# One table function for GELU, and two 64-row matmuls side by side, in a spectral block with a GEGLU feed-forward

## The chip, the cores and the metric

The kernel runs on one core of a Trainium2 chip. The metric is the device time of one execution in microseconds (us), lower is better. The engines are PE (TensorE, matmuls; its weight loads are listed as PEld), DVE (VectorE), ACT (ScalarE), POOL (GpSimd) and SP (SyncE, which here only issues DMAs).

## The reference

Two blocks in sequence, on x of shape 1 x 2048 x 576 in bf16. The first mixes tokens and features with a 2-D Fourier filter; the second is a feed-forward network with a gated GELU.

```python
def _gelu(x):
    return jax.nn.gelu(x, approximate=True)

def _A_ref(x, w_r, w_i):          # S = 2048, D = 576
    X = rfft2(x.astype(float32))
    X = X * (w_r + 1j * w_i)
    return irfft2(X, s=(S, D)).astype(bfloat16)

def _B_ref(x, w_gate, w_up, w_down):   # F = 4608
    return (_gelu(x @ w_gate) * (x @ w_up)) @ w_down

h  = x + _A_ref(_layernorm(x), A_w_r, A_w_i)
h2 = h + _B_ref(_layernorm(h), B_w_gate, B_w_up, B_w_down)
```

The approximate GELU is the tanh form. It equals g times the sigmoid of a cubic in g, which is how the kernel before computes it.

## The kernel before

The kernel is written with a tile framework. The program order is a list of priorities: a scheduler decides the order on each engine ahead of time, allots buffers, inserts the waits, and picks the engine of `nc.any` copies. So instructions of one stage can stand among those of another.

**Stage A, to 178 us.** Tables of sines and cosines are built, x is normalised and transposed, and the Fourier transforms are done as matmuls and DVE butterflies. At the start SP loads x into `h_sb` (L71, four pieces) and the first nine column blocks of the gate weights into `wg_pre` (L84); POOL loads those of the up weights into `wu_pre` (L85). As 576 features are four and a half times 128, the weights have five row blocks (`dt` 0 to 4) and the fifth has only 64 rows. Rows 64 to 127 of the fifth block are set to zero by POOL (L79, L80), so that the fifth matmul may use all 128 rows.

**LN stage, 178 to about 234 us.** For each of the 16 token groups `s2` of 128 tokens: the last inverse transform (`y_ps`, L667 to L690, partly with 33 rows, since 289 frequencies are 128 + 128 + 33), the sum into `h_sb` (L701), the statistics on ACT (L93, L97), the square root on ACT (L111), the normalised row `hrow` on DVE (L710), and five transposes on PE (`pt`, L722), the fifth with 64 columns. Copies (L723) bring these into `hlnT`, which holds the normalised activations with features on partitions. Rows 64 to 127 of its fifth block were set to zero at the start (L73).

**FFN, from 228 us to the end.** Four token chunks `tcnk` of 512 tokens. For each, a loop over the 36 column blocks `f` of 128 hidden features:

- five matmuls of 128 rows, 128 columns and 512 tokens into `gate_ps` (L793), five more into `up_ps` (L801); each of the two has two PSUM buffers;
- GELU in four steps: Square on ACT into `t_sb` (L809), DVE (t + 1/c) times gate into `z_sb` (L811), Sigmoid on ACT into `s_sb` (L815), DVE gate times s (L818);
- times `up_ps` on DVE into `P_sb` (L819).

Then the down projection: eight accumulators `acc` of 288 columns (four groups of 128 tokens, two halves), each over 36 matmuls (L826), and a sum into `h_sb` on DVE (L833). In the order that the scheduler made, some fifty of the 288 down matmuls of a chunk stand between the gate and up matmuls. A buffer of `gate_ps` is given back by L818, one of `up_ps` by L819.

The weights are streamed again for each token chunk, in pieces of up to nine `f`, into two buffers `wg_c` and `wu_c`. For each piece POOL first sets rows 64 to 127 of the fifth block to zero (L757, L758); SP then issues the gate loads (L766, L770) and POOL the up loads (L771, L775). In the first token chunk the pieces are shorter (9, 1, 3, 5, 9 and 9 blocks), and the down weights `wd_sb` (L783) are loaded in it too.

Of the kernel before, what the change touches and what calls it, by code (L numbers as in the profile page):

```python
# [10 lines left out]
ACT = mybir.ActivationFunctionType  # L11
ALU = mybir.AluOpType
FP32 = mybir.dt.float32
BF16 = mybir.dt.bfloat16

P = 128
S = 2048
S2 = 16
D = 576
# [3 lines left out]
DT_SIZES = [128, 128, 128, 128, 64]  # L23
NDT = 5
# [3 lines left out]
GELU_C1 = 2.0 * math.sqrt(2.0 / math.pi)  # L28
GELU_C3 = 0.044715
# [7 lines left out]
def kernel_body(  # L37
# [12 lines left out]
    nc = tc.nc  # L50
# [25 lines left out]
    NPRE = 9  # L76
    wg_pre = xpool.tile([P, NDT, NPRE * P], BF16, name="wg_pre")
    wu_pre = xpool.tile([P, NDT, NPRE * P], BF16, name="wu_pre")
    nc.gpsimd.memset(wg_pre[64:128, NDT - 1, :], 0.0)  # L79
    nc.gpsimd.memset(wu_pre[64:128, NDT - 1, :], 0.0)  # L80
    for dt in range(NDT):
        Kd = DT_SIZES[dt]
        d0 = dt * P
        nc.sync.dma_start(wg_pre[:Kd, dt, :], B_w_gate[d0 : d0 + Kd, 0 : NPRE * P])  # L84
        nc.gpsimd.dma_start(wu_pre[:Kd, dt, :], B_w_up[d0 : d0 + Kd, 0 : NPRE * P])  # L85
    sumsA = small.tile([P, S2], FP32, name="sumsA")
    sumsqA = small.tile([P, S2], FP32, name="sumsqA")
    sumsB = small.tile([P, S2], FP32, name="sumsB")
# [31 lines left out]
    with tc.tile_pool(name="consts", bufs=1) as consts:  # L120
# [230 lines left out]
        with (  # L351
# [262 lines left out]
            with (  # L614
# [30 lines left out]
                for s2 in range(S2):  # L645
                    B2r = bpool.tile([P, NJT, P], BF16, name="B2r", tag="B2r")
                    B2i = bpool.tile([P, NJT, P], BF16, name="B2i", tag="B2i")
                    Gc = G3[:, s2, 0, :]
                    Gs = G3[:, s2, 1, :]
                    Gns = G3[:, s2, 2, :]  # L650
                    for jt in range(1, NJT):
                        Mj = JT_SIZES[jt]
                        j0 = jt * P
                        ur = Ar[:, s2, j0 : j0 + Mj]
                        ui = Ai[:, s2, j0 : j0 + Mj]
                        b2r_ps = psB.tile([P, P], FP32, name="b2r_ps", tag="b2r_ps")
                        b2i_ps = psB.tile([P, P], FP32, name="b2i_ps", tag="b2i_ps")
                        nc.tensor.matmul(b2r_ps[:Mj, :], lhsT=ur, rhs=Gc, start=True, stop=False)  # L658
                        nc.tensor.matmul(b2r_ps[:Mj, :], lhsT=ui, rhs=Gns, start=False, stop=True)  # L659
                        nc.tensor.matmul(b2i_ps[:Mj, :], lhsT=ur, rhs=Gs, start=True, stop=False)  # L660
                        nc.tensor.matmul(b2i_ps[:Mj, :], lhsT=ui, rhs=Gc, start=False, stop=True)
                        nc.any.tensor_copy(B2r[:Mj, jt, :], b2r_ps[:Mj, :])  # L662
                        nc.any.tensor_copy(B2i[:Mj, jt, :], b2i_ps[:Mj, :])
                    for c in range(2):
                        c0 = c * (D // 2)
                        y_ps = psB.tile([P, D // 2], FP32, name="y_ps", tag="y_ps")
                        nc.tensor.matmul(  # L667
                            y_ps[:],
                            lhsT=b2a[:, s2, 0, :],
                            rhs=CDp[:, 0, c0 : c0 + D // 2],  # L670
                            start=True,
                            stop=False,
                        )
                        nc.tensor.matmul(
                            y_ps[:],
                            lhsT=b2a[:, s2, 1, :],
                            rhs=SDp[:, 0, c0 : c0 + D // 2],
                            start=False,
                            stop=False,
                        )  # L680
                        for jt in range(1, NJT):
                            Mj = JT_SIZES[jt]
                            nc.tensor.matmul(  # L683
                                y_ps[:],
                                lhsT=B2r[:Mj, jt, :],
                                rhs=CDp[:Mj, jt, c0 : c0 + D // 2],
                                start=False,
                                stop=False,
                            )
                            nc.tensor.matmul(  # L690
                                y_ps[:],
                                lhsT=B2i[:Mj, jt, :],
                                rhs=SDp[:Mj, jt, c0 : c0 + D // 2],
                                start=False,
                                stop=(jt == NJT - 1),
                            )
                        if "y" in dbg:
                            ydbg = bpool.tile([P, D // 2], FP32, name="ydbg", tag="ydbg")
                            V.tensor_copy(ydbg[:], y_ps[:])
                            nc.sync.dma_start(dbg["y"][:, s2, c0 : c0 + D // 2], ydbg[:])  # L700
                        V.tensor_tensor(  # L701
                            h_sb[:, s2, c0 : c0 + D // 2],
                            h_sb[:, s2, c0 : c0 + D // 2],
                            y_ps[:],
                            ALU.add,
                        )
                    ln_stats(h_sb, s2, sumsB, sumsqB, hpool)
                    rstd1, nmr1 = ln_scalars(sumsB, sumsqB, s2, s2 + 1, hpool)
                    hrow = hpool.tile([P, D], BF16, name="hrow", tag="hrow")
                    V.tensor_scalar(  # L710
                        hrow[:],
                        h_sb[:, s2, :],
                        rstd1[:, s2 : s2 + 1],
                        nmr1[:, s2 : s2 + 1],
                        op0=ALU.mult,
                        op1=ALU.add,
                    )
                    for dt in range(NDT):
                        Kd = DT_SIZES[dt]
                        d0 = dt * P  # L720
                        pt = psT.tile([P, P], BF16, name="pt", tag="pt")
                        nc.tensor.transpose(pt[:Kd, :], hrow[:, d0 : d0 + Kd], ident[:])  # L722
                        nc.any.tensor_copy(hlnT[:Kd, dt, s2 * P : (s2 + 1) * P], pt[:Kd, :])  # L723
    if "h" in dbg:
        nc.sync.dma_start(dbg["h"], h_sb[:])
    if "hlnT" in dbg:
# [2 lines left out]
    with (  # L729
# [14 lines left out]
        for tcnk in range(4):  # L744
# [5 lines left out]
            for qi, (fa, fb) in enumerate(chunks):  # L750
# [3 lines left out]
                if not skip_load:  # L754
                    wg_c = wgpool.tile([P, NDT, FQ * P], BF16, name="wg_c", tag="wg_c")
                    wu_c = wgpool.tile([P, NDT, FQ * P], BF16, name="wu_c", tag="wu_c")
                    nc.gpsimd.memset(wg_c[64:128, NDT - 1, : nfq * P], 0.0)  # L757
                    nc.gpsimd.memset(wu_c[64:128, NDT - 1, : nfq * P], 0.0)  # L758
                    g0 = 0
                    while g0 < nfq:  # L760
                        g1 = min(g0 + 3, nfq)
# [10 lines left out]
                            wu_c[:, 0:4, lc0:lc1],  # L772
                            B_w_up[0 : 4 * P, gc0:gc1].rearrange("(dt k) c -> k dt c", k=P),
                        )
                        nc.gpsimd.dma_start(wu_c[:64, 4, lc0:lc1], B_w_up[4 * P : D, gc0:gc1])  # L775
                        g0 = g1
                if not wd_loaded and (tcnk > 0 or qi >= 1):
                    wd_loaded = True
# [5 lines left out]
                for fi in range(nfq):  # L784
# [4 lines left out]
                        wgs, wus, fi2 = wg_c, wu_c, fi  # L789
                    gate_ps = psG.tile([P, 4 * P], FP32, name="gate_ps", tag="gate_ps")  # L790
                    up_ps = psG.tile([P, 4 * P], FP32, name="up_ps", tag="up_ps")
                    for dt in range(NDT):
                        nc.tensor.matmul(  # L793
                            gate_ps[:],
                            lhsT=wgs[:, dt, fi2 * P : (fi2 + 1) * P],
                            rhs=hlnT[:, dt, tok0 : tok0 + 512],
                            start=(dt == 0),
                            stop=(dt == NDT - 1),
                        )
                    for dt in range(NDT):  # L800
                        nc.tensor.matmul(  # L801
                            up_ps[:],
                            lhsT=wus[:, dt, fi2 * P : (fi2 + 1) * P],
                            rhs=hlnT[:, dt, tok0 : tok0 + 512],
                            start=(dt == 0),
                            stop=(dt == NDT - 1),
                        )
                    t_sb = gpool.tile([P, 4 * P], BF16, name="t_sb", tag="t_sb")
                    nc.scalar.activation(t_sb[:], gate_ps[:], ACT.Square)  # L809
                    z_sb = gpool.tile([P, 4 * P], FP32, name="z_sb", tag="z_sb")  # L810
                    V.scalar_tensor_tensor(  # L811
                        z_sb[:], t_sb[:], 1.0 / GELU_C3, gate_ps[:], op0=ALU.add, op1=ALU.mult
                    )
                    s_sb = gpool.tile([P, 4 * P], BF16, name="s_sb", tag="s_sb")
                    nc.scalar.activation(  # L815
                        s_sb[:], z_sb[:], ACT.Sigmoid, bias=zerob[:], scale=GELU_C1 * GELU_C3
                    )
                    V.tensor_tensor(s_sb[:], gate_ps[:], s_sb[:], ALU.mult)  # L818
                    V.tensor_tensor(P_sb[:, f, :], s_sb[:], up_ps[:], ALU.mult)  # L819
            for st in range(4):  # L820
                s2 = tcnk * 4 + st
# [67 lines left out]
```

## Time and profile before

| | before |
|---|---|
| median of 6 runs | 699.7 us (697.57 to 700.83) |
| the profiled execution | 700.78 us, span 699.0 us |
| granted TensorE clock, mean | 0.938 |
| PE busy | 585.2 us, 84% |
| DVE busy | 478.0 us, 68% |
| ACT busy | 302.5 us, 43% |
| POOL busy | 127.2 us, 18% |

The span runs from the first to the last instruction; the execution's own time is 1.8 us longer. In a row of the profile, L793 is line 793 of the kernel; then come the engine, the operation, out<-in, the shape (for PE rows*columns of the array, then rows x columns that are streamed), the count, the busy time in us, the mean duration of one in ns, and the idle time before it with what ended it. In a timeline the first two numbers are the start and the duration in us. Matmuls are pipelined: the duration is a latency, and the distance from one start to the next is what a matmul takes of the engine.

### The profile page before, as it was taken

Reading aid. Unit: us, or ns where it says so; the run is one execution under the profiler, and the core shown is the slowest. Engines: PE = TensorE matmul, PEld = TensorE weight load, DVE = VectorE, ACT = ScalarE, POOL = GpSimd, SP = SyncE. Lnnn points to the kernel's source line nnn. Section 1 sums busy time; section 2 is a strip of 40 time slices with the busy share of each in tenths; the row PEclk is TensorE's granted clock in tenths of the full one; section 3 lists DMA queues with packets and bytes.
Section 4 is the critical chain, followed back from the end, with each engine's and each line's share of the span. In section 5 each row is a group of like instructions: output and inputs, shape, how many; then the busy total and the mean of one; then the engine's idle time right before and its main releaser. Section 6 shows DMA issues by size and latency. Waiting matters only on the chain.

```text
span 699.0 us, 9591 instructions
## 1 busy us (share of the span) xinstructions
PE 585.2 (84%) x3470; PEld 327.7 (47%) x3502; DVE 478.0 (68%) x1008; ACT 302.5 (43%) x713; POOL 127.2 (18%) x181
## 2 busy tenths in 40 slices
PE   0069980202999999999999999999999999999997
PEld 0037740201455444447744445754444674444475
DVE  5984699999577888882188886148888416878810
ACT  6753591200677655550055553025555104555500
POOL 8910000000000335312002333003213300330000
PEclk9999965655699999999999999999999999999999
DMA  9500000000000958335005553103345500540000
GB/s 309 101 14 1 1 2 0 1 0 0 1 1 1 325 160 246 91 97 149 35 2 152 152 153 97 57 35 99 86 121 153 153 1 35 152 138 17 0 2 34
DMA packets 45294, 55.48 MB, mean 79 GB/s; under 512 B 8992, under 2 KB 37936, under 8 KB 45248
## 3 DMA queue, kind: packets, MB, share of 16 engines
q1 hardware_dynamic: 36720, 29.80, 14.9%
q0 software_dynamic: 8528, 25.08, 12.1%
q8 instruction: 27, 0.44, 0.3%
q14 instruction: 19, 0.16, 0.1%
HBM read 52.50 MB, written 2.36 MB: 78 GB/s over the span
## 4 chain that ended last, share of the span: by engine, by line
DVE 46%; PE 34%; ACT 16%; issue 2%; DMA 1%; DVEq 0%; SPq 0%; ACTq 0%
PE acc L826 17%; ACT s_sb L815 14%; DVE s_sb L818 13%; DVE z_sb L811 12%; DVE P_sb L819 5%; PE gate_ps L793 2%; PE y_ps L683 2%; PE pt_x L345 2%; PE ar_ps L370 2%; PE y_ps L690 2%; PE ai_ps L378 1%; PE up_ps L801 1%; PE pt L722 1%; PE y_ps L667 1%; DMA h_sb<-in_A_x_dram 1%
## 5 line engine op out<-in xcount | busy, mean ns | idle before, releaser
L793 PE MATMUL gate_ps<-hlnT,wg_c 128*128 128x512 bf16 x660 | 166.3, 379 | 3.7 <-DVE s_sb L818 0.5
L801 PE MATMUL up_ps<-hlnT,wu_c 128*128 128x512 bf16 x661 | 166.3, 379 | 0.5
L815 ACT ACTIVATE s_sb<-z_sb,zerob 128x512 bf16<-128x512 f32 x144 | 104.0, 722 | 141.5 <-DVE z_sb L811 141.5
L826 PE MATMUL acc<-wd_sb,P_sb 128*128 128x288 bf16 x1152 | 156.7, 286 | 0.7
L818 DVE TENSOR_TENSOR s_sb<-gate_ps,s_sb 128x512 bf16<-128x512 f32 x144 | 99.6, 692 | 57.4 <-ACT s_sb L815 57.4
L826 PEld LDWEIGHTS <-P_sb 128*128 128x128 bf16 x1152 | 112.1, 98 | 43.5 <-DVE P_sb L819 2.9
L809 ACT ACTIVATE t_sb<-gate_ps 128x512 bf16<-128x512 f32 x144 | 85.1, 591 | 105.8 <-PE gate_ps L793 103.2
L757 POOL MEMSET wg_c<- 64x1152 bf16 (+3 forms) x17 | 16.0, 940 | 492.7 <-issue 302.6
L793 PEld LDWEIGHTS <-wg_c 128*128 128x128 bf16 x675 | 65.7, 97 | 81.2 <-issue 10.8
L819 DVE TENSOR_TENSOR P_sb<-s_sb,up_ps 128x512 bf16<-128x512 bf16 x144 | 98.3, 683 | 5.3
L801 PEld LDWEIGHTS <-wu_c 128*128 128x128 bf16 x675 | 66.0, 98 | 76.6 <-issue 1.3
L811 DVE SCALAR_TENSOR_TENSOR z_sb<-t_sb,gate_ps 128x512 f32<-128x512 bf16 x144 | 98.4, 683 | 4.5 <-ACT t_sb L809 3.9
L833 DVE TENSOR_TENSOR h_sb<-h_sb,acc 128x288 bf16<-128x288 bf16 x32 | 14.5, 454 | 102.3 <-PE acc L826 102.3
L345 PE MATMUL pt_x<-ident,xn 128*128 128x128 bf16 (+1 forms) x80 | 14.0, 293 | 40.9 <-DVE xn L256 36.4
L658 PE MATMUL b2r_ps<-G_105,Ar 128*128 128x128 bf16 (+1 forms) x32 | 7.9, 247 | 42.8 <-DVE Ar L547 42.8
L771 POOL DMA_DIRECT2D wu_c<-in_B_w_up_dram x46 | 35.3, 768 | 1.4 <-issue 1.4
L345 PEld LDWEIGHTS <-xn 128*128 128x128 bf16 (+1 forms) x80 | 7.5, 128 | 47.2 <-DVE xn L256 36.4
L662 ACT CAST B2r<-b2r_ps 128x128 bf16<-128x128 f32 (+1 forms) x22 | 5.8, 263 | 49.1 <-PE b2r_ps L659 48.9
L658 PEld LDWEIGHTS <-Ar 128*128 128x128 bf16 (+1 forms) x32 | 3.2, 100 | 47.5 <-DVE Ar L547 43.0
L775 POOL DMA_DIRECT2D wu_c<-in_B_w_up_dram x46 | 25.0, 544 | 0.0
L564 POOL DMA_DIRECT2D wi_all<-in_A_w_i_dram x32 | 23.1, 730 | 2.1 <-DMA wu_pre<-in_B_w_up_dram 1.0
L701 DVE TENSOR_TENSOR h_sb<-h_sb,y_ps 128x288 bf16<-128x288 bf16 x32 | 14.4, 451 | 11.2 <-PE y_ps L690 10.8
(396 smaller groups left out, 675.7 us busy)
## 6 DMA issues: line engine op xcount, KB each, us to landing
wg_c<-in_B_w_gate_dram SPq DMA_DIRECT2D x44, 384.0 KB, 5.2
wu_c<-in_B_w_up_dram POOLq DMA_DIRECT2D x44, 384.0 KB, 7.4
wd_sb<-in_B_w_down_dram SPq DMA_DIRECT2D x2, 1296.0 KB, 14.3
wd_sb<-in_B_w_down_dram POOLq DMA_DIRECT2D x2, 1296.0 KB, 11.7
h_sb<-in_A_x_dram SPq DMA_DIRECT2D x4, 576.0 KB, 5.8
out_dram<-h_sb SPq DMA_DIRECT2D x4, 576.0 KB, 2.8
wu_c<-in_B_w_up_dram POOLq DMA_DIRECT2D x44, 48.0 KB, 6.9
wg_c<-in_B_w_gate_dram SPq DMA_DIRECT2D x44, 48.0 KB, 4.8
```

Of the source, the lines that this page charges most:

```text
L345: nc.tensor.transpose(pt[:Kd, :], xn[:, s2, d0 : d0 + Kd], ident[:])
L564: nc.gpsimd.dma_start(wi_all[:, p, :], A_w_i[k2 * P : (k2 + 1) * P, ja:jb])
L771: nc.gpsimd.dma_start(wu_c[:, 0:4, lc0:lc1], B_w_up[0 : 4 * P, gc0:gc1].rearrange("(dt k) c -> k dt c", k=P),)
L775: nc.gpsimd.dma_start(wu_c[:64, 4, lc0:lc1], B_w_up[4 * P : D, gc0:gc1])
L793: nc.tensor.matmul(gate_ps[:], lhsT=wgs[:, dt, fi2 * P : (fi2 + 1) * P], rhs=hlnT[:, dt, tok0 : tok0 + 512], start=(dt == 0), stop=(dt == ...
L801: nc.tensor.matmul(up_ps[:], lhsT=wus[:, dt, fi2 * P : (fi2 + 1) * P], rhs=hlnT[:, dt, tok0 : tok0 + 512], start=(dt == 0), stop=(dt == ND ...
L809: nc.scalar.activation(t_sb[:], gate_ps[:], ACT.Square)
L811: V.scalar_tensor_tensor(z_sb[:], t_sb[:], 1.0 / GELU_C3, gate_ps[:], op0=ALU.add, op1=ALU.mult)
L815: nc.scalar.activation(s_sb[:], z_sb[:], ACT.Sigmoid, bias=zerob[:], scale=GELU_C1 * GELU_C3)
L818: V.tensor_tensor(s_sb[:], gate_ps[:], s_sb[:], ALU.mult)
L819: V.tensor_tensor(P_sb[:, f, :], s_sb[:], up_ps[:], ALU.mult)
L826: nc.tensor.matmul(acc[:], lhsT=P_sb[:, f, st * P : (st + 1) * P], rhs=wd_sb[:, f, cc0 : cc0 + D // 2], start=(f == 0), stop=(f == NFT - 1),)
```

## The change

GELU becomes one table function on ACT, `Gelu_apprx_tanh`, read from `gate_ps` and written to `s_sb`; Square, the two DVE steps and Sigmoid go. The gate's 64-row rest stays in rows 0 to 63 of the fifth weight block, the up's is loaded into rows 64 to 127, and no rows are set to zero for the weights any more. `hrow` is widened to 640 columns, and a DVE copy repeats its last 64 features, so that the fifth transpose gives 128 rows: features 512 to 575 twice, in rows 0 to 63 and 64 to 127 of `hlnT`'s fifth block. The first two matmuls of each `f` are then the two 64-row rests, gate in the upper half of the array's rows and up in the lower half, and eight 128-row matmuls follow.

```diff
-    nc.gpsimd.memset(wg_pre[64:128, NDT - 1, :], 0.0)
-    nc.gpsimd.memset(wu_pre[64:128, NDT - 1, :], 0.0)
     for dt in range(NDT):
...
-        nc.gpsimd.dma_start(wu_pre[:Kd, dt, :], B_w_up[d0 : d0 + Kd, 0 : NPRE * P])
+        uo = 64 if dt == NDT - 1 else 0
+        nc.gpsimd.dma_start(wu_pre[uo : uo + Kd, dt, :], B_w_up[d0 : d0 + Kd, 0 : NPRE * P])
...
-                    hrow = hpool.tile([P, D], BF16, name="hrow", tag="hrow")
+                    hrow = hpool.tile([P, NDT * P], BF16, name="hrow", tag="hrow")
                     V.tensor_scalar(
-                        hrow[:],
+                        hrow[:, 0:D],
...
+                    V.tensor_copy(hrow[:, D : NDT * P], hrow[:, 4 * P : D])
                     for dt in range(NDT):
-                        Kd = DT_SIZES[dt]
                         d0 = dt * P
                         pt = psT.tile([P, P], BF16, name="pt", tag="pt")
-                        nc.tensor.transpose(pt[:Kd, :], hrow[:, d0 : d0 + Kd], ident[:])
-                        nc.any.tensor_copy(hlnT[:Kd, dt, s2 * P : (s2 + 1) * P], pt[:Kd, :])
+                        nc.tensor.transpose(pt[:], hrow[:, d0 : d0 + P], ident[:])
+                        nc.any.tensor_copy(hlnT[:, dt, s2 * P : (s2 + 1) * P], pt[:])
...
-                    nc.gpsimd.memset(wg_c[64:128, NDT - 1, : nfq * P], 0.0)
-                    nc.gpsimd.memset(wu_c[64:128, NDT - 1, : nfq * P], 0.0)
...
-                        nc.gpsimd.dma_start(wu_c[:64, 4, lc0:lc1], B_w_up[4 * P : D, gc0:gc1])
+                        nc.gpsimd.dma_start(wu_c[64:128, 4, lc0:lc1], B_w_up[4 * P : D, gc0:gc1])
...
-                    for dt in range(NDT):
+                    fs = slice(fi2 * P, (fi2 + 1) * P)
+                    ts = slice(tok0, tok0 + 512)
+                    nc.tensor.matmul(
+                        gate_ps[:], lhsT=wgs[0:64, 4, fs], rhs=hlnT[0:64, 4, ts], start=True, stop=False
+                    )
+                    nc.tensor.matmul(
+                        up_ps[:], lhsT=wus[64:128, 4, fs], rhs=hlnT[64:128, 4, ts], start=True, stop=False
+                    )
+                    for dt in range(4):
                         nc.tensor.matmul(
...
+                            gate_ps[:], lhsT=wgs[:, dt, fs], rhs=hlnT[:, dt, ts], start=False, stop=(dt == 3)
+                        )
+                    for dt in range(4):
                         nc.tensor.matmul(
...
+                            up_ps[:], lhsT=wus[:, dt, fs], rhs=hlnT[:, dt, ts], start=False, stop=(dt == 3)
+                        )
-                    t_sb = gpool.tile([P, 4 * P], BF16, name="t_sb", tag="t_sb")
-                    nc.scalar.activation(t_sb[:], gate_ps[:], ACT.Square)
-                    z_sb = gpool.tile([P, 4 * P], FP32, name="z_sb", tag="z_sb")
-                    V.scalar_tensor_tensor(
-                        z_sb[:], t_sb[:], 1.0 / GELU_C3, gate_ps[:], op0=ALU.add, op1=ALU.mult
-                    )
                     s_sb = gpool.tile([P, 4 * P], BF16, name="s_sb", tag="s_sb")
-                    nc.scalar.activation(
-                        s_sb[:], z_sb[:], ACT.Sigmoid, bias=zerob[:], scale=GELU_C1 * GELU_C3
-                    )
-                    V.tensor_tensor(s_sb[:], gate_ps[:], s_sb[:], ALU.mult)
+                    nc.scalar.activation(s_sb[:], gate_ps[:], ACT.Gelu_apprx_tanh, bias=zerob[:], scale=1.0)
                     V.tensor_tensor(P_sb[:, f, :], s_sb[:], up_ps[:], ALU.mult)
```

More of the change, by code (lines that the diff above doesn't have):

```diff
@@ L791, in kernel_body @@
                     up_ps = psG.tile([P, 4 * P], FP32, name="up_ps", tag="up_ps")
-                    for dt in range(NDT):
[L793 to L798, printed above, removed]
+                    fs = slice(fi2 * P, (fi2 + 1) * P)
+                    ts = slice(tok0, tok0 + 512)
@@ L799, in kernel_body @@
                         )
-                    for dt in range(NDT):
+                    for dt in range(4):
                         nc.tensor.matmul(
[L802 to L806, printed above, removed]
-                        )
-                    t_sb = gpool.tile([P, 4 * P], BF16, name="t_sb", tag="t_sb")
```

## The prediction

> **What bounds the kernel now.** I read the page first, for the groups that cost most.
>
> ```profile
> PE 585.2 (84%) x3470; PEld 327.7 (47%) x3502; DVE 478.0 (68%) x1008; ACT 302.5 (43%) x713; POOL 127.2 (18%) x181
> ...
> L793 PE MATMUL gate_ps<-hlnT,wg_c 128*128 128x512 bf16 x660 | 166.3, 379 | 3.7 <-DVE s_sb L818 0.5
> L801 PE MATMUL up_ps<-hlnT,wu_c 128*128 128x512 bf16 x661 | 166.3, 379 | 0.5
> ...
> L818 DVE TENSOR_TENSOR s_sb<-gate_ps,s_sb 128x512 bf16<-128x512 f32 x144 | 99.6, 692 | 57.4 <-ACT s_sb L815 57.4
> ```
>
> The FFN (gate, up, GELU, down) runs from 228 us to the end. PE's 379 ns is the latency of one pipelined matmul, so its occupancy has to be read from start to start. The chain of waits puts most of the loop on DVE and ACT, as if the GELU set its pace; the table of windows (PE, PEld, DVE, ACT, POOL, clock, DMA share, GB/s) speaks against that: PE has hardly a gap, DVE is busy for 63%.
>
> ```profile
> 178.00:228.00 50.00, 49.52 (x350) 25.52 (x349) 33.76 (x168) 37.55 (x142) 0.48 (x3) 0.92 0.01 1
> 345.00:462.00 117.00, 115.63 (x647) 63.72 (x655) 73.25 (x116) 46.25 (x72) 23.82 (x32) 1.00 0.33 97
> ```
>
> The timeline of PE then shows what is lost inside the loop:
>
> ```profile
> 403.92 0.41 PE L826 MATMUL acc<-wd_sb,P_sb 128*128 128x288 bf16 x2
> 404.39 1.24 PE L793 MATMUL gate_ps<-hlnT,wg_c 128*128 128x512 bf16 x5
> 405.47 0.29 PE L826 MATMUL acc<-wd_sb,P_sb 128*128 128x288 bf16 x1
> 405.59 1.24 PE L801 MATMUL up_ps<-hlnT,wu_c 128*128 128x512 bf16 x5
> ```
>
> Five 512-column matmuls take 1.08 us (404.39 to 405.47), 0.216 each; a 288-column one takes 0.12. Down-projection matmuls fill places where PE would wait. Two of them end at 404.16, but the gate starts at 404.39: gate_ps has two buffers, and the older one is free only after DVE's third GELU step (L818). The list of waits has it as
>
> ```profile
> ACT s_sb L815 <- DVE z_sb L811: 141.5, 143, 1.5
> PEld L793 <- issue: 11.4, 44, 0.4
> ```
>
> The long first line costs nothing (ACT is not the bound); the second, 11.4 us in 44 waits of 0.25, is time that PE loses.
>
> The check by sums: one token chunk lasts from 345.85 to 462.07, 116.2 us. It holds 360 x 0.216 = 77.8 us of gate and up and 288 x 0.123 = 35.4 of down (0.123 from 28.6 us for 232 in the chain), 113.2 together. So only 3.0 us per chunk, 12 in all, is waiting; the rest is PE's own work. The five-step GELU is late by a hair, not by its length.
>
> Last, what a change of tile shape costs PE. The LN stage already has 33-row matmuls between 128-row ones, and 64-column transposes:
>
> ```profile
> 205.04 0.30 PE L667 MATMUL y_ps<-CDp,b2a 128*128 128x288 bf16 x1
> 205.26 0.24 PE L722 MATMUL pt<-ident,hrow 128*64 128x128 bf16 x1
> 205.44 0.30 PE L674 MATMUL y_ps<-SDp,b2a 128*128 128x288 bf16 x1
> 205.57 0.29 PE L683 MATMUL y_ps<-CDp,B2r 128*128 128x288 bf16 x1
> 205.69 0.29 PE L690 MATMUL y_ps<-SDp,B2i 128*128 128x288 bf16 x1
> 205.91 0.29 PE L683 MATMUL y_ps<-CDp,B2r 33*128 33x288 bf16 x1
> 206.14 0.30 PE L667 MATMUL y_ps<-CDp,b2a 128*128 128x288 bf16 x1
> ```
>
> Equal shapes: 205.57 to 205.69, 0.12. Into 33 rows: 0.22. Out again: 0.23. Each change costs 0.10 us.
>
> **The change, part by part.** Everything is summed against the profiled execution, 700.78 us (span 699.0), which is 1.1 above the median of 699.7.
>
> *GELU.* Per f it removes the Square on ACT (591 ns), two DVE passes (683 and 692) and the Sigmoid (722), and adds one Gelu from PSUM, bounded by the two ACT rows at 0.6 to 0.72. None of this lies on PE. What it buys is gate_ps: free 0.7 us after the gate's last matmul instead of 3. DVE and ACT then need 0.7 us each in a 2.16 us period; PE stops waiting. That returns the 12 us of waits, less a remnant: **-11.0** (bounds -8 to -12.5). Next late is nothing but PE. The down matmuls used as fillers move to the end of the chunk, at the same price.
>
> *The row pair.* Two 64-row matmuls replace two 128-row ones. If they run side by side, one 0.216 disappears: 144 x 0.216 = -31.1. But the tile shape changes twice per f: 144 x 0.20 = +28.8. And the second starts a little after the first. No row shows two different row tiles; the nearest, two 33-row matmuls on the same rows (starts at 193.06 and 193.19 us), is serial: 0.13 apart for 288 columns, 0.216 for 512. The Trainium skill ("TensorE: Matmul & The Clock Gate", Measured speedup vs the span model) says that a pack lasts one matmul plus about 4 ns for each further tile: +0.6 in all, against +31.1 by the row. I depart from the nearest row because its two matmuls share rows, so it can't tell. I take 40 ns, since the second weight load must also come after the change of shape (back-to-back 128-column loads with their matmuls are 55 to 60 ns apart at 207.5 to 207.8): +5.8. The same skill's page "TensorEngine Tiling (Array Packing)" promises up to 2x for a contraction of 64, but under Key Properties that changing mode drains the array; by the first alone this part gives -31, with the 0.10 rows it gives -31.1 + 28.8 + 5.8 = **+3.5** (bounds -3 to +29).
>
> The up matmul of the pair also moves ahead of four gate matmuls. It needs up_ps (free about 0.75 us after up of f-2, that is over 1 us early) and its weights about 2 us sooner. Tightest is f=13 in the first chunk: the up loads that POOL issues from 253.7 have landed at 259.8, and up starts at 261.0; now it would be wanted near 259. The memset ahead of them on POOL's queue goes, so they start some 0.6 us earlier: I take nothing, bound +1.
>
> *Memsets.* 28 of the larger ones (1.05 us each) leave POOL, which is 18% busy and which no PE wait names: 0. But at the start two of them delay wu_pre's DMAs to 5.35 us. These will be issued 2.1 us sooner, beside the x loads on SP's queue, whose third piece lands at 7.96 and starts the ACT statistics at 7.98, on the chain. Shared bandwidth: **+0.5** (0 to +1.5).
>
> *LN stage.* Here too PE is the bound (window 178 to 228). The 16 transposes of 64 columns become 128 wide; 13 of them stand alone between other shapes and each costs 0.22 - 0.12 going in and 0.18 - 0.06 coming out, 0.22 in all: up to -2.8. Added are 16 DVE copies of 128x64, bounded by 0.14 (128x1 ops) and 0.22 (128x128 copy), on an engine busy 34 of 50 us; only the fifth transpose needs them. If the cover fails, +2.5. I take **-1.5**.
>
> *Table loads.* At the hand-over ACT runs:
>
> ```profile
> 229.68 0.60 ACT L809 ACTIVATE t_sb<-gate_ps 128x512 bf16<-128x512 f32 x1
> 230.17 0.28 ACT L111 ACTIVATE ln_std<-ln_var,epsb 128x1 f32<-128x1 f32 x1
> 231.19 1.28 ACT L815 ACT_TABLE_LOAD   x1
> ```
>
> Square needed no load, so it could pass ahead of the last Sqrt. Gelu in its place would load its table, then Sqrt loads again, then Gelu: two loads more, 2.6 us, which PE sees only through the last transposes: **+1.5** (0 to +4).
>
> Sum: -11.0 + 3.5 + 0.5 - 1.5 + 1.5 = **-7.0**. 700.8 - 7.0 = 693.8; against the median, 692.7.
>
> **The rivals.** *The pair is serial* (the weight load of the second tile or its stream waits for the first). Then the row part is +28.8 and the sum is -11 + 28.8 + 0.5 = 18.3 up, 718 (LN stage and table loads cancel). For it: nothing in the trace shows two tiles at once. Against it: the skill's measured packs. It decides from 0.05 us more per f than I took (7.0 / 144), so even a half-overlap brings the kernel back to 700. *The pair comes apart*: if the order puts the up half elsewhere, four changes of shape per f and no overlap: 144 x 0.40 = +57.6, less 11, 746. Against it: with one DVE step per f both buffers are free long before. *Free of charge*: the page's 4 ns, the full -12.5 and all of the transposes: -12.5 - 1.7 - 2.8 = -17, 683. *The GELU was the bound* (as the chain of waits reads): then DVE's 57.4 us of waiting would come back; the sums exclude it, since PE's own work is 113.2 of 116.2.
>
> **How the numbers follow.** About 0.3%, 2 us, is what a measurement can tell from no change. My case, 686 to 698: 0.58, of which 0.05 lies within 2 us of before. Free of charge, 680 to 686: 0.06. Half-overlap or a dearer change, 698 to 708: 0.18, a fourth of it within 2 us. Serial, 708 to 722: 0.13. Apart: 0.05. So faster 0.59, same 0.09, slower 0.32. The range 684 to 718 leaves out the pair coming apart and a tail on each side.
>
> **What would show it.** Right: PE gaps before the gate gone; first 64-row matmul 0.31 after its predecessor; the second within 0.06 of it; the next 128-row matmul 0.31 later; a chunk of 114 us instead of 116.2. Wrong: a pair 0.2 apart, 64-row matmuls apart from each other, or PE still waiting for gate_ps or for weights.

## The result, and the profile after

The changed kernel takes 681.3 us (median of 10 runs, 679.66 to 682.89) against 699.9 for the kernel before: ratio 0.974, 95% interval 0.9726 to 0.9754. It is 18.6 us faster; I had forecast 7 us and a range down to 684. The profiled execution took 682.67 us, span 680.9.

On the page, PE's share of the span stayed at 84% (its busy time fell by 15.7 us, with the span), while DVE lost 179 us and ACT 85:

```profile
PE 569.5 (84%) x3470; PEld 302.6 (44%) x3502; DVE 298.6 (44%) x733; ACT 217.5 (32%) x572; POOL 95.2 (14%) x145
...
PE 77%; DVE 16%; DMA 3%; issue 2%; ACT 1%; SPq 0%; POOL 0%; DVEq 0%
...
L794 PE MATMUL up_ps<-hlnT,wu_c 64*128 64x512 bf16 x135 | 52.2, 387 | 0.1
L791 PE MATMUL gate_ps<-hlnT,wg_c 64*128 64x512 bf16 x135 | 52.2, 387 | 0.0
```

The second line is the chain that ended last. Before, it was DVE 46%, PE 34%, ACT 16%, although PE was nearly full; now that DVE and ACT have room it reads as it should. The 64-row rows show 387 ns each, a latency; that they run side by side is not in them but in the timeline of PE:

```profile
395.60 0.38 PE L802 MATMUL up_ps<-hlnT,wu_c 128*128 128x512 bf16 x1
395.91 0.39 PE L791 MATMUL gate_ps<-hlnT,wg_c 64*128 64x512 bf16 x1
395.92 0.39 PE L794 MATMUL up_ps<-hlnT,wu_c 64*128 64x512 bf16 x1
396.23 1.04 PE L798 MATMUL gate_ps<-hlnT,wg_c 128*128 128x512 bf16 x4
397.11 1.03 PE L802 MATMUL up_ps<-hlnT,wu_c 128*128 128x512 bf16 x4
398.07 0.39 PE L791 MATMUL gate_ps<-hlnT,wg_c 64*128 64x512 bf16 x1
```

Last 128-row matmul to the pair: 0.31 (0.216 and 0.10 for the change of shape). The two of the pair: 0.01 or less; the trace's nanoseconds give 3 to 4. Pair to the next 128-row matmul: 0.31 to 0.32. One f: 395.91 to 398.07, 2.155 us by the nanoseconds, against ten times 0.216 = 2.16 before.

The token chunks, from the table of windows (the first number after the stretch is its length; then PE, PEld, DVE, ACT, POOL, clock, DMA share, GB/s):

```profile
302.35:415.21 112.86, 111.59 (x641) 56.87 (x648) 28.38 (x44) 24.79 (x37) 15.62 (x24) 1.00 0.34 100
```

A stretch from the first down matmul of one chunk to that of the next is 112.86 us. PE's work in it is 36 x 2.155 = 77.6 plus 288 x 0.1225 = 35.3 for down, 112.9: no waiting is left. Before it was 116.22.

Where the 18.1 us of span went, by the starts of the first instructions of each stage:

| stretch | before | after | difference |
|---|---|---|---|
| start, to the first transpose of xn | 36.44 | 34.10 | -2.3 |
| rest of stage A, to the first transpose of hrow | 149.27 | 149.07 | -0.2 |
| LN stage, to the first gate matmul | 42.19 | 40.08 | -2.1 |
| first token chunk, to its last down matmul | 117.62 | 114.25 | -3.4 |
| three more chunks | 3 x 116.22 | 3 x 112.86 | -10.1 |
| tail | 4.8 | 4.8 | 0 |

### The profile page after: what moved, and what is told of

Read it like the earlier page. It is cut to its first block, busy times and chain, and to the rows that moved or that the text cites. A ratio compares the mean times of both kernels' runs of the same rounds, so it can differ in the third digit from the quotient of the medians.

```text
span 680.9 us, 9020 instructions
## 1 busy us (share of the span) xinstructions
PE 569.5 (84%) x3470; PEld 302.6 (44%) x3502; DVE 298.6 (44%) x733; ACT 217.5 (32%) x572; POOL 95.2 (14%) x145
## 4 chain that ended last, share of the span: by engine, by line
PE 77%; DVE 16%; DMA 3%; issue 2%; ACT 1%; SPq 0%; POOL 0%; DVEq 0%
PE acc L814 21%; PE gate_ps L798 19%; PE up_ps L802 17%; PE gate_ps L791 6%; PE y_ps L682 2%; PE pt_x L344 2%; PE ar_ps L369 2%; PE y_ps L689 2%; PE ai_ps L377 1%; PE pt L721 1%; DMA h_sb<-in_A_x_dram 1%; PE y_ps L666 1%; DMA wu_c<-in_B_w_up_dram 1%; DMA wg_c<-in_B_w_gate_dram 1%; DVE xn L255 1%
## 5 line engine op out<-in xcount | busy, mean ns | idle before, releaser
L806 ACT ACTIVATE s_sb<-gate_ps,zerob 128x512 bf16<-128x512 f32 x144 | 99.1, 688 | 314.6 <-PE gate_ps L798 314.5
L814 PE MATMUL acc<-wd_sb,P_sb 128*128 128x288 bf16 x1152 | 141.8, 286 | 0.0
L802 PE MATMUL up_ps<-hlnT,wu_c 128*128 128x512 bf16 x540 | 138.6, 379 | 0.0
L798 PE MATMUL gate_ps<-hlnT,wg_c 128*128 128x512 bf16 x510 | 133.2, 381 | 4.8 <-issue 4.6
L768 POOL DMA_DIRECT2D wu_c<-in_B_w_up_dram x46 | 35.3, 768 | 509.0 <-PE up_ps L802 303.5
L802 PEld LDWEIGHTS <-wu_c 128*128 128x128 bf16 x540 | 52.8, 98 | 63.7
L798 PEld LDWEIGHTS <-wg_c 128*128 128x128 bf16 x540 | 41.7, 97 | 62.5 <-issue 29.7
L794 PE MATMUL up_ps<-hlnT,wu_c 64*128 64x512 bf16 x135 | 52.2, 387 | 0.1
L791 PE MATMUL gate_ps<-hlnT,wg_c 64*128 64x512 bf16 x135 | 52.2, 387 | 0.0
L791 PEld LDWEIGHTS <-wg_c 64*128 64x128 bf16 x135 | 12.5, 92 | 56.6 <-issue 55.8
L689 PE MATMUL y_ps<-SDp,B2i 128*128 128x288 bf16 (+1 forms) x64 | 19.8, 321 | 0.3 <-DVE B2i L662 0.3
L682 PE MATMUL y_ps<-CDp,B2r 128*128 128x288 bf16 (+1 forms) x64 | 20.1, 320 | 0.0
```

The costliest lines, as they stand in the source:

```text
L682: nc.tensor.matmul(y_ps[:], lhsT=B2r[:Mj, jt, :], rhs=CDp[:Mj, jt, c0 : c0 + D // 2], start=False, stop=False,)
L689: nc.tensor.matmul(y_ps[:], lhsT=B2i[:Mj, jt, :], rhs=SDp[:Mj, jt, c0 : c0 + D // 2], start=False, stop=(jt == NJT - 1),)
L768: nc.gpsimd.dma_start(wu_c[:, 0:4, lc0:lc1], B_w_up[0 : 4 * P, gc0:gc1].rearrange("(dt k) c -> k dt c", k=P),)
L791: nc.tensor.matmul(gate_ps[:], lhsT=wgs[0:64, 4, fs], rhs=hlnT[0:64, 4, ts], start=True, stop=False)
L794: nc.tensor.matmul(up_ps[:], lhsT=wus[64:128, 4, fs], rhs=hlnT[64:128, 4, ts], start=True, stop=False)
L798: nc.tensor.matmul(gate_ps[:], lhsT=wgs[:, dt, fs], rhs=hlnT[:, dt, ts], start=False, stop=(dt == 3))
```

## The experiments

Theory A, from the trace: PE's own work is the bound of the FFN; the GELU part gains only the waits for `gate_ps`; the row pair gives back to changes of shape what it gains by overlap; the rest comes from the start and the LN stage. Theory B: the overlap of the pair gives the gain. Theory C: GELU was the bound. All runs are timed against the kernel before on the same chip (medians of before 699.5 to 700.0).

| run | time us | ratio, 95% interval | a later token chunk us |
|---|---|---|---|
| after | 681.3 | 0.974 (0.9726 to 0.9754) | 112.86 |
| e1, GELU alone | 687.6 | 0.983 (0.9812 to 0.9848) | 112.98 |
| e2, pair and the rest without GELU | 740.0 | 1.0576 (1.0555 to 1.0597) | 127.23 |
| e3, memsets back | 684.2 | 0.9776 (0.9756 to 0.9796) | 112.86 |
| e4, pair on the same rows | 712.8 | 1.0187 (1.0172 to 1.0203) | 120.48 |
| e5, pairs two by two | 667.9 | 0.9531 (0.9507 to 0.9556) | 109.02 |
| e6, pairs in threes | 660.3 | 0.9448 (0.943 to 0.9466) | 107.76 |
| e7, wide transposes alone | 697.1 | 0.997 (0.9957 to 0.9983) | 116.17 |
| e9, before with three PSUM buffers | 687.5 | 0.9829 (0.9813 to 0.9846) | 112.98 |
| e10, e2 with three PSUM buffers | 684.4 | 0.9773 (0.9753 to 0.9793) | 113.5 |
| e11, memsets later | 697.8 | 0.9967 (0.9954 to 0.9981) | 116.2 |

**The GELU alone (e1).** The kernel before, with

```diff
-                    nc.scalar.activation(t_sb[:], gate_ps[:], ACT.Square)
...
-                    V.tensor_tensor(s_sb[:], gate_ps[:], s_sb[:], ALU.mult)
+                    nc.scalar.activation(s_sb[:], gate_ps[:], ACT.Gelu_apprx_tanh, bias=zerob[:], scale=1.0)
```

> The kernel before with only the GELU made one table function; ten 128-row matmuls per f and the zeroed rows stay. Theory A (PE's own work bounds the FFN, the five-step GELU only held gate_ps too long): a token chunk falls from 116.2 us to 360 x 0.2158 + 288 x 0.1225 = 113.0, the start and the LN stage stay: 699.9 - 13 = 687. Theory B (the gain of the change is mostly the overlap of the two 64-row matmuls): the chunk keeps most of its length, 694 or more. Theory C (GELU was the bound, the chain of waits read literally): far below 680.

687.6, and a chunk of 112.98. So the row pair is worth 112.98 - 112.86 = 0.12 us per chunk, half a microsecond in all, and theory B falls. ACT's wait list confirms what became idle: ACT now waits for PE, once per f.

```profile
ACT s_sb L809 <- PE gate_ps L793: 312.6, 141, 36.8
```

**One more PSUM buffer, old GELU (e9).** `psG` with `bufs=3` instead of 2, nothing else.

> The kernel before, unchanged but for three PSUM buffers instead of two for gate_ps and up_ps. Theory A (the five-step GELU cost time only because gate_ps was given back late): most of the 13 us of waits go, a chunk of about 113.3 us, 688 to 690. Rival (DVE's three passes of 0.685 us per f, 2.06 of 2.16 us, can't keep up when PE doesn't wait): 695 to 700.

687.5, the same as e1 within the spread, and the same chunk of 112.98. The timeline of PE has no hole ahead of the gate any more:

```profile
399.98 1.24 PE L793 MATMUL gate_ps<-hlnT,wg_c 128*128 128x512 bf16 x5
401.05 1.24 PE L801 MATMUL up_ps<-hlnT,wu_c 128*128 128x512 bf16 x5
402.13 1.24 PE L793 MATMUL gate_ps<-hlnT,wg_c 128*128 128x512 bf16 x5
```

DVE still has its three passes per f here. This settles the matter against theory C, and shows what the table function bought: not arithmetic, but the early return of a buffer.

**The pair without the GELU (e2, e10).** The changed kernel with the old GELU (its four steps ahead of the product with `up_ps`) put back; in e10 with three PSUM buffers as well.

> The changed kernel with the five-step GELU put back; row pair, wide transposes and no memsets stay. In the scheduler's order of this program the pair stands apart: gate rest, four gate matmuls, up rest, four up matmuls, with down matmuls between as before. Theory A: per f ten matmuls of 0.216 and four changes of shape of 0.10, so 2.56 us instead of 2.155, 144 x 0.40 = +58 over the changed kernel, and little waiting for gate_ps is left since PE is slower: 735 to 745. Theory B (overlap gives the gain): 690 to 697.

> The changed kernel with the five-step GELU put back and three PSUM buffers each for gate_ps and up_ps, so that in the scheduler's order the pair stands together again. Theory A (the pair came apart in the two-buffer version only because up_ps was given back after gate_ps; DVE's 2.06 us per f still fit under PE's 2.155): chunks of 113 us, 681 to 684. Rival (DVE's three passes and the five-step chain become the bound beside a PE that no longer waits): 690 or more, with PE waiting for gate_ps.

e2 takes 740.0. In its planned order the two rests of an f stand apart. The likely reason, argued from the code and supported by e10: up_ps comes free one DVE pass after gate_ps, so the up rest misses its place beside the gate rest. The timeline of PE in e2:

```profile
402.80 0.41 PE L823 MATMUL acc<-wd_sb,P_sb 128*128 128x288 bf16 x2
403.14 0.39 PE L791 MATMUL gate_ps<-hlnT,wg_c 64*128 64x512 bf16 x1
403.46 1.04 PE L798 MATMUL gate_ps<-hlnT,wg_c 128*128 128x512 bf16 x4
404.33 0.29 PE L823 MATMUL acc<-wd_sb,P_sb 128*128 128x288 bf16 x1
404.55 0.39 PE L794 MATMUL up_ps<-hlnT,wu_c 64*128 64x512 bf16 x1
404.87 0.39 PE L802 MATMUL up_ps<-hlnT,wu_c 128*128 128x512 bf16 x1
```

Each rest stands alone, 0.32 of its own and 0.10 added to what is ahead of it. A chunk is 14.37 us longer than in the changed kernel, 57.5 in four. With the third buffer (e10) most pairs stand together again, a chunk is 113.5, the time 684.4, just above the 681 to 684 that I gave it. In three of the 36 f of a later chunk the up rest still comes 0.20 to 0.25 us late, with no other matmul in between:

```profile
404.34 0.39 PE L791 MATMUL gate_ps<-hlnT,wg_c 64*128 64x512 bf16 x1
404.59 0.37 PE L794 MATMUL up_ps<-hlnT,wu_c 64*128 64x512 bf16 x1
```

These three make up the 0.64 us by which the chunk is longer than that of the changed kernel; what the up rest waits for there, the trace does not name. So the two halves of the change are not independent: with two buffers, it is the new GELU that keeps the pair a pair.

**Is the overlap real (e4)?** The up rest in rows 0 to 63 as well:

```diff
-                        up_ps[:], lhsT=wus[64:128, 4, fs], rhs=hlnT[64:128, 4, ts], start=True, stop=False
+                        up_ps[:], lhsT=wus[0:64, 4, fs], rhs=hlnT[0:64, 4, ts], start=True, stop=False
```

(and the up weights loaded there).

> The changed kernel with the up rest in rows 0 to 63 too, so that both 64-row matmuls use the same rows of the array; the number of changes of shape is the same. Theory A (the two run at the same time, 3 ns apart): the second starts 0.216 to 0.23 later instead, 144 x 0.215 = +31, 712. Rival (the overlap hides nothing, the change of shape would have taken the time anyway): 681 to 690.

712.8. The timeline of PE:

```profile
401.69 0.39 PE L791 MATMUL gate_ps<-hlnT,wg_c 64*128 64x512 bf16 x1
401.92 0.38 PE L794 MATMUL up_ps<-hlnT,wu_c 64*128 64x512 bf16 x1
402.22 0.39 PE L798 MATMUL gate_ps<-hlnT,wg_c 128*128 128x512 bf16 x1
```

On the same rows the second starts 0.23 later, on other rows 3 to 4 ns later. The overlap is worth 4 x (120.48 - 112.86) = 30.5 us. The changes of shape take back all but about half a microsecond of it (e1 against the changed kernel).

**Fewer changes of shape (e5, e6).** In e5 the pair of an even f closes its accumulation, so that it stands beside the opening pair of the next:

```diff
+                    late = f % 2 == 0
...
+                    if not late:
+                        rest(True)
...
+                    if late:
+                        rest(False)
```

In e6 the same for three f (one closing, two opening), with `psG` at three buffers and the weights looked up two f ahead.

> The changed kernel with the pair of every even f moved to the end of its accumulation, so that it stands next to the pair of the following f: two changes of shape per two f instead of four. Theory A (0.10 us for each change of shape on PE's path): 144 changes fewer, 14.4 us, 681.3 - 14.4 = 667, less about 0.3 for the second pair starting behind the first. Rival (gate_ps, finished later for even f, holds PE up, or the change of shape is hidden): 675 to 685.

> The changed kernel with the pairs of three consecutive f side by side (one closing, two opening) and three PSUM buffers each for gate_ps and up_ps: two changes of shape per three f instead of six. Theory A: 192 changes fewer, 19.2 us, 662, the first f of each chunk somewhat later. Rival (loads of weights wanted up to two f earlier, or PSUM buffers, hold PE up): 667 to 675, no better than two by two.

667.9 and 660.3. The timeline of PE in e6:

```profile
400.95 0.39 PE L806 MATMUL gate_ps<-hlnT,wg_c 64*128 64x512 bf16 x1
400.95 0.39 PE L809 MATMUL up_ps<-hlnT,wu_c 64*128 64x512 bf16 x1
401.18 0.38 PE L806 MATMUL gate_ps<-hlnT,wg_c 64*128 64x512 bf16 x1
401.18 0.38 PE L809 MATMUL up_ps<-hlnT,wu_c 64*128 64x512 bf16 x1
401.39 0.38 PE L806 MATMUL gate_ps<-hlnT,wg_c 64*128 64x512 bf16 x1
401.40 0.38 PE L809 MATMUL up_ps<-hlnT,wu_c 64*128 64x512 bf16 x1
401.70 1.04 PE L820 MATMUL gate_ps<-hlnT,wg_c 128*128 128x512 bf16 x4
```

Pairs on pairs are 0.22 apart, as plain matmuls are, and the price is paid at the two ends. Per change saved: e5 4 x (112.86 - 109.02) / 144 = 0.107 us, e6 4 x (112.86 - 107.76) / 192 = 0.106. The price of 0.10 read from the LN stage was some 6% too low. e6 beats both kernels: 5.5% under before.

**The LN stage alone (e7).** The kernel before with `hrow` at 640 columns, the DVE copy, and five 128-wide transposes.

> The kernel before with only the LN stage's part of the change: hrow of 640 columns, its DVE copy, and the fifth transpose 128 wide (the repeated rows meet zero weights). Theory A (PE is the bound there, a lone 64-column transpose costs 0.22 us of shape changes): the time from the first transpose of hrow to the first gate matmul falls from 42.2 to about 40.1 us, 697.8. Rival (DVE's extra copy takes it back; the 2.1 us came from the new order at the hand-over to the FFN): 699.5 to 701.

697.1. The first transposes of hrow and the first gate matmuls, from the views of `pt` and of `gate_ps`:

```profile
L722 PE MATMUL pt<-ident,hrow x80: 216/219/230, 184.2 to 228.9; 128*128 128x128 bf16 x80
L793 PE MATMUL gate_ps<-hlnT,wg_pre x45: 376/379/379, 224.2 to 244.4; 128*128 128x512 bf16 x45
```

From the first transpose of hrow to the first gate matmul it takes 39.9 us (184.24 to 224.16) instead of 42.2. Some 0.3 of this is probably the clock: e1 and e9 have the LN stage of before and take 41.9, with full clock from the start of the stage, while before had half clock in its first half microsecond. Three of the narrow transposes of before stand behind the first gate matmul, and e7's first token chunk is 0.7 us shorter (116.9 against 117.6). Together that is 2.7 to 3.0 us, as much as the changes of shape around the narrow transposes were priced at (2.8): they were on the path, and the 16 copies on DVE are covered.

**The start (e3, e11).** In e3 the changed kernel gets two memsets of the old size back, on rows of `wg_pre` and `wu_pre` that it doesn't use; in e11 the kernel before has its own two behind the five iotas.

> The changed kernel with two memsets of the same size put back on POOL at the start, on the rows of wg_pre and wu_pre that it doesn't use. Theory A (without the memsets POOL's iotas come 2 us sooner, so the scheduler placed a DVE product of 1.67 us into DVE's wait for the ACT statistics, 2.9 us before and 0.6 after): the first transpose returns from 34.1 to about 36.4 us and the time to 683.6. Theory B (the order on DVE moved for another reason, or the memsets cost only through DMA sharing): 681.3 within 0.5.

> The kernel before with the two memsets of wg_pre and wu_pre placed on POOL behind the five iotas instead of ahead of wu_pre's loads; nothing else. Theory A (the start gains because the iotas come earlier and the scheduler can put DVE's product of 1.67 us into DVE's wait for ACT): first transpose at 34.1 instead of 36.4 us, 697.5. Rival (the gain needs the memsets gone, not moved): first transpose at 36 or later, 699.5 to 700.5.

684.2 and 697.8, and the first transposes of xn at 36.46 and 34.14 us. Moving the memsets is enough. What moved with them is the order on DVE. The timeline of DVE, before:

```profile
13.96 1.23 DVE L208 TENSOR_SCALAR kr_t_133<-prod_t_131 128x2048 f32<-128x2048 f32 x1
18.10 0.17 DVE L238 TENSOR_SCALAR mvA<-sumsA 128x8 f32<-128x8 f32 x1 [2.92 <-ACT ln_junk L93]
18.19 1.67 DVE L286 TENSOR_TENSOR prod_cd<-vdc,jrow 128x1445 f32<-128x1445 f32 x1
```

and after:

```profile
13.93 1.23 DVE L207 TENSOR_SCALAR kr_t_131<-prod_t_129 128x2048 f32<-128x2048 f32 x1
15.07 1.66 DVE L285 TENSOR_TENSOR prod_cd<-vdc,jrow 128x1445 f32<-128x1445 f32 x1
16.65 1.22 DVE L208 TENSOR_SCALAR kr_t_131<-kr_t_131 128x2048 f32<-128x2048 f32 x1
18.48 0.17 DVE L237 TENSOR_SCALAR mvA<-sumsA 128x8 f32<-128x8 f32 x1 [0.61 <-ACT ln_junk L92]
```

A hole of 2.92 us on DVE, waiting for ACT's statistics, became one of 0.61. Two independent DVE instructions were put ahead of the wait. In e11 they stand there too:

```profile
15.11 1.66 DVE L284 TENSOR_TENSOR prod_cd<-vdc,jrow 128x1445 f32<-128x1445 f32 x1
18.51 0.17 DVE L236 TENSOR_SCALAR mvA<-sumsA 128x8 f32<-128x8 f32 x1 [0.57 <-ACT ln_junk L91]
```

That the memsets' place decides this is shown (e11); why is only argued: one of the two needs an iota (jrow) that stood behind the memsets on POOL, so it may have come too late in the scheduler's plan. On the chip that iota was done at 9 us before and at 6.7 after, long before the wait began at 15.

## Why the prediction was wrong

The bound was read rightly: PE is full, the GELU gives back only waits, the pair's overlap is real and is eaten by two changes of shape. The sum failed by 11.1 us, all but 0.2 of it in five terms that were off in the same direction. Two of them had a wrong mechanism, the late start of the pair's second matmul and the memsets; the table loads did not come; the other two had a wrong size. Two measured values lie outside the bounds that I gave: the GELU (bound -12.5) and the memsets (bound 0).

- *The row pair, +3.5.* The step that failed is the second matmul's later start, taken as 40 ns because its weight load "must also come after the change of shape". It does come after it, but beside the first: in the trace of the changed kernel the two weight loads start 4 ns apart, and so do the two matmuls. This is the 4 ns of the Trainium skill ("TensorE: Matmul & The Clock Gate", Measured speedup vs the span model), which I had quoted and then raised tenfold. So +5.8 becomes +0.5. The changes of shape cost a little more than the 28.8 I gave them: by the trace's nanoseconds 0.312 going in, 0.319 coming out, and 0.226 to the matmul after that, where 0.216 each would stand without them, 30.1 in all. -31.1 + 30.1 + 0.5 = -0.5; measured: -0.5 (e1 against after).
- *GELU, -11.0.* It gave -13.0, 4 x 3.24. I valued a down matmul at 0.123 from a stretch of the chain that contains the full latency of its last matmul; start to start it is 0.1225, and a 512-column one is a little under 0.216. So the waits were 3.24 us per chunk and not 3.0. And I kept a remnant of waiting for which there was no ground.
- *Memsets, +0.5.* It gave -2.3: the wrong sign. What I named of the cost did come (by ACT's start the third piece of x landed 0.4 us later, at 8.35 instead of 7.98; whether by shared bandwidth was not tested). I left out that a scheduler re-plans the neighbours of what is removed. The 2.92 us hole on DVE was in the trace, on the path, with independent work right behind it.
- *Table loads, +1.5.* Nothing: in the changed kernel the last Sqrt (224.97) runs ahead of the first Gelu's table load (225.63), so there are six loads, as before. The wide transposes alone don't bring this order: in e7 the first Square (225.59) still runs ahead of the last Sqrt (226.09). All runs with the row pair have it; why was not tested. In e1, where Gelu came first, the two further loads do appear. The timeline of ACT in e1:

```profile
228.72 1.28 ACT L809 ACT_TABLE_LOAD   x1
230.01 0.69 ACT L809 ACTIVATE s_sb<-gate_ps,zerob 128x512 bf16<-128x512 f32 x1
230.72 1.28 ACT L111 ACT_TABLE_LOAD   x1
232.01 0.30 ACT L111 ACTIVATE ln_std<-ln_var,epsb 128x1 f32<-128x1 f32 x1
232.33 1.28 ACT L809 ACT_TABLE_LOAD   x1
```

  Even there the first token chunk is only 2.0 us longer than a later one, against 1.4 before, so they cost some 0.6 us there.
- *LN stage, -1.5.* It gave -2.1 up to the first gate matmul. The term was -2.8 with half of it withheld for no measured reason; e7 shows that all of it can be had.

The measured terms, -13.0 - 0.5 - 2.3 - 2.1 and -0.2 in stage A, make -18.1, the difference of the spans. Among the rivals, "free of charge" stood at 683 with a chance of 0.06. The time came close to it in part by luck: the 4 ns and the full waits were its reasons too, but it had 1.2 us too much for the row pair, 0.7 too much for the transposes, and nothing for the start, which gave 2.3. The serial pair was priced at 718 and measured 712.8 where the other terms were present (e4); the pair coming apart was priced at +57.6 and measured 4 x (127.23 - 112.98) = +57.0 (e2 against e1). I had argued against that rival that both buffers are free long before; with two buffers this holds only because the GELU came with it.

One small risk that I had put at nothing, with a bound of +1, did come: the up weights of f = 13 in the first chunk were late, and the up rest stood 0.46 us behind the gate rest. Its weight load in the changed kernel:

```profile
252.42 0.39 PE L791 MATMUL gate_ps<-hlnT,wg_c 64*128 64x512 bf16 x1
252.88 0.09 PEld L794 LDWEIGHTS <-wu_c 64*128 64x128 bf16 x1 [0.37 <-DMA wu_c<-in_B_w_up_dram]
```

In the table of stretches this stands in the first token chunk, against the 0.7 us that the wide transposes gain there.

## What to carry to other kernels

Read PE from start to start and compare the sum of its work with the stage's length before believing a chain of waits: here 113 of 116 us were PE's own, and a third PSUM buffer bought what the new GELU bought (e9). Row tiles pay only if several matmuls share one change of shape: with a single pair between two changes the gain was 0.5 us, with three pairs 21 us (both against e1). When a program's order is planned, removing an instruction can re-plan its neighbours: look for holes on the path with ready work behind them, and expect both signs (one new order gained 2.3 us here, that of e2 lost 57).

## What the runs showed of the hardware

Two 64-row matmuls on different rows start 3 to 4 ns apart and do not slow each other: the next 128-row matmul follows 0.32 us later, as after a single one (0.32 in e2). On the same rows they are 0.23 apart (e4). A change of shape cost 0.10 to 0.12 us of PE where rows changed (128 to 64 or 33) and where columns did (128 to 64), going in and coming out.

The time from the first transpose of xn to the first of hrow was between 146.5 and 149.3 us in these kernels. From 87 to 167 us, where DVE is busy for over 99% of the time, the mean granted TensorE clock is 0.54 to 0.61, and it returns to full speed at different moments. The table of windows over the same stretch, after and then e10:

```profile
177.00:184.00 7.00, 7.00 (x36) 3.51 (x34) 2.80 (x16) 4.42 (x11) 0.00 (x0) 0.53 0.00 0
```

```profile
177.00:184.00 7.00, 6.70 (x52) 3.58 (x52) 4.96 (x28) 5.27 (x20) 0.00 (x0) 0.91 0.01 2
```

The clock is 0.53 in the one and 0.91 in the other, and e10 reaches the LN stage 2.7 us earlier. Executions of one and the same kernel differ too: of the 15 runs of the kernel before that were timed beside e11, two had a mean clock of 0.941 and took 697.9 us, the other thirteen, at 0.938 to 0.939, took 698.9 to 700.9. So the length of each stage says more than the span of a single execution, which can differ by 2 us from what the medians say (e3's profiled span is only 0.8 us over that of after, its median 2.9). What sets the moment was not tried.
